# g_norm loaded as a row, chunk 3 token-major: a linear-attention and SoLU kernel with a new order table

## The chip, the cores and the metric

The kernel runs on one core of a Trainium2 chip. The metric is the device time of one execution in microseconds (us): the median of 3 runs is 185.53 us (184.94 to 195.7). One further execution was recorded by the profiler, and every row and time line below is from that one.

The engines are named as in the profile: PE is TensorE (matmuls; PEld its weight loads), DVE is VectorE, ACT is ScalarE, POOL is GpSimd and SP is SyncE, which here only issues transfers.

## The reference

```python
# attention: q, k, v are (8 batches, 8 heads, 576 tokens, 64)
kv  = einsum('bhsd,bhse->bhde', k, v)
out = einsum('bhsd,bhde->bhse', q, kv)
out = out / sqrt(mean(out * out, axis=-1) + 1e-6) * g_norm
x   = out.transpose(0, 2, 1, 3).reshape(4608, 512)
# feed-forward: w_in (512, 1024), w_out (1024, 512)
h    = x @ w_in
e    = exp(h - max(h))
solu = h * e / (sum(e) + 1e-9)
mu, var = mean(solu), mean((solu - mu) ** 2)          # over 1024
y    = ((solu - mu) / sqrt(var + 1e-6) * g_ln) @ w_out
```

All inputs and the result are float32; the kernel computes the matmuls in bfloat16. It leaves the division by the sum of exponentials and the subtraction of the mean out of the large tensors: u = h * exp(h) is multiplied with a w_out whose columns are scaled by g_ln and centred, and one factor per token, made from the sums of u, of its squares and of the exponentials, scales the result.

## The kernel before

**Chunks.** The 4608 tokens are cut into nine chunks of 512: chunks 0 to 7 hold 512 tokens of one batch each, chunk 8 the 64 that are left of every batch. Batches 0 and 1 are loaded in two halves of four heads, the others whole. For the first half of batch 0, q, k and v go through staging tiles that SP loads in float32; all other loads are issued by POOL, which converts to bfloat16 on the way. POOL also issues w_in, w_out and the last tokens of q (`q_last`).

**Attention** of chunk c: `kv_mm` (L376, PE) makes the k-v products of a batch, and copies on DVE or ACT bring them to `kvd`. q is turned, by PE and a copy for chunks 0 to 3 (`qT_mm`, L414), by a DMA transpose that SP issues for chunks 4 to 8 (`qT`, L422). `o_mm` (L433) is the attention product, in two halves. Then, four times per chunk: a square on ACT (`sq`, L236), a mean over the head by a matmul (`s_mm`, L445), the reciprocal root on ACT (`ln` and `ex`, L449 and L453; one instruction, L459, in chunk 0), and `x` on DVE (L465), which multiplies the attention output by the root and by g_norm. For that g_norm stands in a column of 128 partitions, `g_rep`, twice the 64 values; two DMAs write it (L294, L295). g_ln is loaded as eight rows (L293), turned on PE (`turn_g`, L287) and copied by DVE (`g_ln`, L290).

**Feed-forward, feature-major** (chunks 0 to 3): `h` (L502) makes 128 features by 512 tokens with four matmuls, `exp` on ACT (L509), `u` on DVE (L513). For the sums, POOL squares u (`usq`, L238, now and then on ACT, L236) and adds pairs of exponentials (`es`, L526); then 80 narrow matmuls (`sums`, L612) add over features, and a few short DVE instructions (`turn`, `stats`, L619 to L629) make the variance. The output matmuls (`out`, L692) take u as it is.

**Token-major** (chunks 4 to 8, `TOKS`): `h` (L530) makes 128 tokens by 512 features with four matmuls. `expt` on ACT (L538) gives the sum of the exponentials with it, in an accumulator that is read by an instruction of its own. `ut` is on DVE (L544), and `bn` (L550, batch-norm statistics, one per tile of 512) and `stats` (L555 to L561) on DVE replace squares, pair sums and `sums`. u has to be turned for the output: two DMA transposes per chunk on SP (`turnu`, L566).

`rstd` (L633, L635) makes the factor on ACT, `ob` scales the output on DVE or ACT (L244, L242), and SP or ACT stores it.

**Order.** Every piece is a word in `ORDER`, such as `h.5.2.0` or `kv_mm.7.0`, with `:act` where it goes to ACT. `Plan.emit` issues the pieces in exactly that order, so each engine works through its own in the order of the table, and a piece whose input is late holds up all behind it on that engine. `HOME` says which of the eight PSUM banks each product uses, and the tiles have few buffers (k, v, q and qT three, x and u two, e and ob four). `warm` pieces are fillers (`FILL`): matmuls of zeros that PE works on, `("s.warm", 19, 512)` being 19 of them, 512 columns wide, into the bank of that name.

Of the kernel before, what the change touches and what calls it, by code (L numbers as in the profile page):

```python
# [8 lines left out]
FP32 = mybir.dt.float32  # L9
# [26 lines left out]
sq.2.0.1 v.4.0 u.1.7 usq.1.7 qT_mm.3.0 w_center.4 u.1.1 usq.1.6 h.1.2.1 exp.1.2 es.1.1 w_center.7 u.1.2 sums.0 qT.3.0
s_mm.2.0.0 turn.0 ln.2.0.0 ex.2.0.0 out.0.0.2 out.0.0.3 k.4.0 stats.0 out.0.2.0 s_mm.2.0.1 ln.2.0.1 out.0.2.1
out.0.2.2 x.2.0.0 usq.1.2 ex.2.0.1 x.2.0.1 rstd.0 ob.0.0 out.0.3.0 out.0.3.1 o_mm.2.1 sq.2.1.0 kv_mm.3.0 kv.3.0.1
kv.3.1.2 sq.2.1.1 qT_mm.3.1 kv.3.0.0:act kv.3.1.0:act store.0.0 out.0.2.3 kv.3.0.2 ob.0.2 store.0.2 s_mm.2.1.0
out.0.3.2 out.0.3.3 ln.2.1.0 h.2.6.0 s_mm.2.1.1 ob.0.3:act qT.3.1 ex.2.1.0 x.2.1.0 ln.2.1.1 ex.2.1.1 usq.1.5 out.0.1.0  # L40
out.0.1.1 x.2.1.1 out.0.1.2 out.0.1.3 ob.0.1:act store.0.3 h.2.1.0 usq.1.1 kv.3.1.1:act h.2.7.0 kv_mm.4.0 kv.4.1.0:act
kv.4.0.2:act o_mm.3.0 kv.4.0.1:act sq.3.0.0 kv.4.1.1 h.2.1.1 kv.4.1.2 kv.4.0.0 q.4.0 h.2.7.1 h.2.3.0 qT.4 es.1.3
h.2.6.1 exp.2.7 exp.2.6 u.2.7 es.1.0 usq.1.3 h.2.0.0 u.2.6 exp.2.1 u.2.1 h.2.0.1 exp.2.0 u.2.0 h.2.3.1 h.2.5.0 exp.2.3
u.2.3 s_mm.3.0.0 k.5.0 h.2.2.0 ln.3.0.0 h.2.4.0 h.2.2.1 h.2.5.1 ex.3.0.0 x.3.0.0 v.5.0 usq.2.7 exp.2.2 exp.2.5 h.2.4.1
u.2.5 usq.2.5 sq.3.0.1 sums.1 turn.1 stats.1 es.2.3 u.2.2 o_mm.3.1 sq.3.1.0 store.0.1 exp.2.4 out.1.2.0 out.1.2.1
# [5 lines left out]
usq.3.0 x.4.0.1 store.1.1 exp.3.2 u.3.1 h.3.7.1 o_mm.4.1 kv_mm.7.0 exp.3.7 u.3.7 sq.4.1.1 es.3.0 kv.7.1.2 out.2.3.0
u.3.2 usq.2.0 kv.7.0.1 usq.2.6 ex.4.0.0 store.1.0 sq.4.1.0 s_mm.4.1.1 ln.4.1.1 usq.2.1 kv.7.1.0:act v.6.0 out.2.3.1
q.6.0 h.3.3.1 kv.7.1.1 ex.4.1.1 qT.6 kv.7.0.0 es.3.2 exp.3.3 q_last.4 x.4.0.0 u.3.3 s_mm.4.1.0 ln.4.1.0 x.4.1.1
kv.7.0.2:act sums.2 o_mm.5.1 turn.2 stats.2 usq.3.6:act ex.4.1.0 x.4.1.0 o_mm.5.0 sq.5.0.0 sq.5.0.1 es.3.3 rstd.2
sq.5.1.0 ob.2.3 out.2.2.0 out.2.0.0 out.2.0.1 ob.2.0 s_mm.5.0.1 store.2.3 out.2.2.1 ob.2.2 ln.5.0.1 ex.5.0.1 x.5.0.1
s_mm.5.0.0 ln.5.0.0 ex.5.0.0 k.6.0 usq.3.2 usq.3.4 s_mm.5.1.0 h.4.0.1 out.2.1.0 out.2.1.1 ln.5.1.0 expt.4.0.1 ut.4.0.1
es.3.1 x.5.0.0 ex.5.1.0 x.5.1.0 h.4.0.0 usq.3.3 q_last.2 expt.4.0.0 ut.4.0.0 sq.5.1.1 h.4.1.1 expt.4.1.1 ut.4.1.1
h.4.3.1 bn.4.0.1 h.4.2.0 kv_mm.6.0 kv.6.0.1 kv.6.1.2 kv.6.0.2 expt.4.3.1 ob.2.1:act kv.6.0.0 kv.6.1.0 ut.4.3.1
s_mm.5.1.1 q_last.5 ln.5.1.1 h.4.3.0 expt.4.3.0 ut.4.3.0 ex.5.1.1 out.3.0.0 usq.3.7 h.4.1.0 kv.6.1.1 expt.4.1.0
usq.3.5 usq.3.1 ut.4.1.0 sums.3 turn.3 stats.3 expt.4.2.0 o_mm.6.1 sq.6.1.1 sq.6.1.0 x.5.1.1 h.4.2.1 expt.4.2.1  # L60
# [117 lines left out]
def kernel(  # L178
# [13 lines left out]
    nc = tc.nc  # L192
# [595 lines left out]
```

## Time and profile before

| what | value |
|---|---|
| median of 3 runs | 185.53 us (184.94 to 195.7) |
| the profiled execution | 187.05 us, of which 185.2 us are the span from the first to the last instruction |
| granted TensorE clock, mean over the span | 0.978 |
| DVE, ACT, POOL busy | 136.0, 141.3, 81.7 us |
| `usq` on POOL, `es` on POOL | 31 of 1040 ns, 16 of 1272 ns |
| `bn` on DVE | 40 of 682 ns |
| median time from issue to landing of a transpose of q, of u | 8.2 us, 3.9 us |
| HBM read, written | 32.51 MB, 9.44 MB |

How to read it: a line of digits gives 40 equal slices of the span (4.63 us each), each digit the busy share in tenths. A line of a window gives its bounds, its length, then for each engine the busy time and in brackets the number of instructions, then the granted clock as a share of the full one, the mean busy share of the 16 DMA engines and the GB/s moved. A line of waits reads: the engine and piece that waited, an arrow to what it waited for, us in total, times, and the longest. A line of the chain gives the start, the length and the piece that the end of the span hung on. A line of a DMA issue gives the count, the KB of each and the us from issue to landing.

### The profile page before, as it was taken

To read this page: it belongs to the slowest core of one execution; us is meant where nothing else is said; L and a number is where in the kernel's file an instruction comes from. 1 tells how busy PE (TensorE), PEld (TensorE's weight loads), DVE (VectorE), ACT (ScalarE), POOL (GpSimd) and SP (SyncE) were. 2 spreads that over 40 slices of the span, in tenths; PEclk is the share of its full clock that TensorE was granted. 3 is DMA by queue.
4 is the path that set the end of the run, shared out by engine and by line. 5 is a ranking of instruction groups with operands and counts; after the bars stand their busy time and mean duration, and the time that the engine had idled before them with its cause. 6 is when DMAs were issued, how large, how long until landed. Compare 5 with 4: busy or idle time off the path is not lost.

```text
span 185.2 us, 4994 instructions
## 1 busy us (share of the span) xinstructions
PE 172.4 (93%) x1996; PEld 86.2 (47%) x2019; DVE 136.0 (73%) x281; ACT 141.3 (76%) x281; POOL 81.7 (44%) x94
## 2 busy tenths in 40 slices
PE   7959999999996999986999999999999999999992
PEld 2545546545453454433544554444444444444451
DVE  1132879999974774673676989799999799988921
ACT  2205999998885989993899879989998987636541
POOL 7832169989999259959999600000000000000000
PEclk9997999999999999996999999999999999999998
DMA  5999999999999999999999996995977394199984
GB/s 191 277 156 206 223 306 321 207 170 190 195 155 240 185 170 167 204 137 264 173 219 137 211 225 98 271 208 127 224 162 172 70 235 96 43 255 212 237 224 169
DMA packets 55320, 35.80 MB, mean 193 GB/s; under 512 B 37240, under 2 KB 49024, under 8 KB 55296
## 3 DMA queue, kind: packets, MB, share of 16 engines
q0 software_dynamic: 17264, 16.45, 54.8%
q1 hardware_dynamic: 37600, 18.36, 43.8%
q10 hardware_dynamic: 432, 0.66, 1.0%
q8 instruction: 16, 0.26, 0.6%
q14 instruction: 8, 0.07, 0.1%
HBM read 32.51 MB, written 9.44 MB: 227 GB/s over the span
## 4 chain that ended last, share of the span: by engine, by line
PE 60%; DMA 14%; POOL 10%; DVE 7%; issue 4%; ACT 3%; POOLq 0%; DVEq 0%
PE out_ps L692 27%; PE h_ps L530 19%; DMA v_sb<-in_v_dram 10%; PE h_ps L502 5%; DMA k_sb<-in_k_dram 4%; POOL usq_sb L238 4%; POOL es_sb L526 3%; PE s_ps L445 3%; PE misc_ps L376 2%; ACT e_sb L509 2%; DVE x_sb L465 2%; PE o_ps L433 2%; DVE misc_ps L663 2%; DVE u_sb L513 1%; POOL k_sb L312 1%
## 5 line engine op out<-in xcount | busy, mean ns | idle before, releaser
L238 POOL TENSOR_TENSOR usq_sb<-u_sb 128x512 bf16<-128x512 bf16 x31 | 31.7, 1040 | 13.8 <-DVE u_sb L513 11.5
L530 PE MATMUL h_ps<-w_in_sb,x_sb 128*128 128x512 bf16 x156 | 37.3, 379 | 0.2
L692 PE MATMUL out_ps<-w_out_sb,w_sb 128*128 128x512 bf16 (+1 forms) x163 | 36.1, 369 | 0.3
L465 DVE SCALAR_TENSOR_TENSOR x_sb<-o_ps,g_rep,rst_sb 128x512 bf16<-128x512 f32 x36 | 26.3, 745 | 9.3 <-ACT rst_sb L453 7.6
L538 ACT ACTIVATE e_sb<-h_ps,zero_t 128x512 f32<-128x512 f32 x40 | 27.2, 685 | 6.2 <-PE h_ps L530 6.1
L692 PE MATMUL out_ps<-w_out_sb,u_sb 128*128 128x512 bf16 x122 | 30.8, 385 | 0.6 <-issue 0.2
L502 PE MATMUL h_ps<-x_sb,w_in_sb 128*128 128x512 bf16 x122 | 29.8, 379 | 0.6 <-issue 0.5
L544 DVE TENSOR_TENSOR u_sb<-h_ps,e_sb 128x512 bf16<-128x512 f32 x40 | 26.4, 682 | 4.3 <-ACT e_sb L538 4.2
L449 ACT ACTIVATE lss_sb<-s_ps,eps_t 128x512 f32<-128x512 f32 x32 | 21.9, 685 | 6.7 <-PE s_ps L445 6.5
L550 DVE BATCH_NORM_STATS2 bn_sb<-u_sb 128x6 f32<-128x512 bf16 x40 | 25.8, 682 | 0.2
L692 PEld LDWEIGHTS <-w_sb 128*128 128x128 bf16 x168 | 16.3, 98 | 18.1 <-issue 0.2
L513 DVE TENSOR_TENSOR u_sb<-h_ps,e_sb 128x512 bf16<-128x512 f32 x32 | 20.9, 684 | 4.7 <-ACT e_sb L509 4.7
L236 ACT ACTIVATE osq_sb<-o_ps,zero_t 128x512 bf16<-128x512 f32 x36 | 23.5, 683 | 0.8 <-PE o_ps L433 0.4
L530 PEld LDWEIGHTS <-x_sb 128*128 128x128 bf16 x160 | 15.4, 98 | 18.6 <-issue 0.6
L453 ACT ACTIVATE rst_sb<-lss_sb,zero_t 128x512 f32<-128x512 f32 x32 | 22.8, 722 | 0.6
L509 ACT ACTIVATE e_sb<-h_ps,zero_t 128x512 f32<-128x512 f32 x32 | 20.5, 689 | 1.2 <-PE h_ps L502 0.7
L526 POOL TENSOR_TENSOR es_sb<-e_sb 128x512 bf16<-128x512 f32 x16 | 20.3, 1272 | 1.0 <-ACT e_sb L509 0.9
L692 PEld LDWEIGHTS <-u_sb 128*128 128x128 bf16 x128 | 12.5, 100 | 15.2 <-issue 1.7
L242 ACT ACTIVATE ob_sb<-out_ps,rstd_sb 128x512 f32<-128x512 f32 (+1 forms) x20 | 13.5, 675 | 6.8 <-PE out_ps L692 3.4
L502 PEld LDWEIGHTS <-w_in_sb 128*128 128x128 bf16 x128 | 11.9, 98 | 13.8 <-issue 0.6
L244 DVE TENSOR_SCALAR ob_sb<-out_ps,rstd_sb 128x512 f32<-128x512 f32 (+1 forms) x17 | 12.2, 730 | 6.6 <-PE out_ps L692 3.8
L376 PE MATMUL misc_ps<-v_sb,k_sb 64*64 64x64 bf16 x720 | 8.7, 203 | 5.6 <-DMA v_sb<-in_v_dram 4.2
(75 smaller groups left out, 171.8 us busy)
## 6 DMA issues: line engine op xcount, KB each, us to landing
out_dram<-ob_sb SPq DMA_DIRECT2D x65, 128.0 KB, 2.8
k_sb<-in_k_dram POOLq DMA_DIRECT2D x6, 576.0 KB, 8.0
v_sb<-in_v_dram POOLq DMA_DIRECT2D x6, 576.0 KB, 7.9
q_sb<-in_q_dram POOLq DMA_DIRECT2D x6, 512.0 KB, 7.8
w_sb<-in_moe_w_out_dram POOLq DMA_DIRECT2D x2, 1024.0 KB, 14.5
w_in_sb<-in_moe_w_in_dram POOLq DMA_DIRECT2D x2, 512.0 KB, 13.9
k_sb<-in_k_dram POOLq DMA_DIRECT2D x3, 288.0 KB, 15.1
v_sb<-in_v_dram POOLq DMA_DIRECT2D x3, 288.0 KB, 14.0
```

Source lines behind the costliest of these rows:

```text
L236: nc.scalar.activation(out=dst, in_=src, func=AF.Square, bias=zero_t[:, :])
L238: on[engine].tensor_tensor(out=dst, in0=src, in1=src, op=MUL)
L453: nc.scalar.activation(out=t.rearrange("p a b c -> p (a b c)"), in_=T["lss", i][:, :], func=AF.Exp, scale=-0.5, bias=zero_t[:, :])
L465: nc.vector.scalar_tensor_tensor(out=t[:, 2 * hf:2 * hf + 2, z], in0=T["o", c, hf, z][:, :, :, :], scalar=g_rep[:, :], in1=T["rst", (c, hf ...
L502: nc.tensor.matmul(bank(("h", c, f), [128, 512])[:, :], w_in_sb[:, dt, f * 128:(f + 1) * 128], T["x", c][:, dt].rearrange("p a b c -> p (a ...
L509: nc.scalar.activation(out=t[:, f % 2, :], in_=T["h", c, f][:, :], func=AF.Exp, bias=zero_t[:, :])
L526: on[engine].tensor_tensor(out=t[:, n, :], in0=e[:, 0, :], in1=e[:, 1, :], op=ADD)
L530: nc.tensor.matmul(bank(("h", c, m, g), [128, 512])[:, :], T["x", c][:, dt, m // 2, 2 * (m % 2):2 * (m % 2) + 2, :].rearrange("p b c -> p ...
L538: nc.scalar.activation(out=t[:, g, :], in_=T["h", c, m, g][:, :], func=AF.Exp, bias=zero_t[:, :], accum_out=se[:, m, g:g + 1])
L544: nc.vector.tensor_tensor(out=t[:, m, g * 512:(g + 1) * 512], in0=T["h", c, m, g][:, :], in1=T["e", c, m][:, g, :], op=MUL)
L550: nc.vector.bn_stats(out=t[:, m, g, :], in_=T["u", c][:, m, g * 512:(g + 1) * 512])
L692: nc.tensor.matmul(bank(key, [128, d_model])[:, cols], T["w", c][:, m, f, :] if c in TOKS else T["u", c][:, f, m * 128:(m + 1) * 128], w_o ...
```

## The change

g_norm is no longer written into a column by DMA. It is loaded twice, as a row of 64, into a ninth row beside the eight of g_ln; the turn on PE takes all nine rows, and one copy on DVE gives `g_cols`, whose columns 0 to 7 are g_ln and whose column 8 is g_norm. `x` now needs that copy (`g_ln`) instead of the loads (`gs`).

`TOKS` gains chunk 3: its feed-forward goes the token-major way, with eight `bn`, two `turnu` and no `usq`, `es` and `sums`. Its q is still turned on PE. The order table, the bank table and the fillers are new throughout: 9 filler pieces instead of 13. Among what moves: SP issues the small loads ahead of q's staging load; POOL issues k, q and v of the second half of batch 0, then k and v of batch 1's first half, then both halves of w_in, and only then q of batch 1; the first attention product stands ahead of the second `kv_mm` of batch 0; `kv_mm.5` and `kv_mm.7` stand ahead of `o_mm.3.1` and `o_mm.4.0`; and the stores of chunk 0 stand behind `qT.4` on SP.

```diff
-q.0.1 warm.0 ld.v ld.k k.0.0 v.0.0:act ld.q ident q.0.0 k.0.1 gs warm.1 kv_mm.0.0 v.0.1 warm.4 qT_mm.0.0 kv.0.0.1:act
+warm.3 k.0.1 warm.0 ld.k ld.v q.0.1 warm.2 gs k.0.0 ident warm.1 v.0.1 ld.q v.0.0:act kv_mm.0.0 q.0.0 kv.0.0.1 k.1.0
+qT_mm.0.0 v.1.0 qT_mm.0.1 qT.0.0 kv.0.0.0 o_mm.0.0 w_in.0 kv_mm.0.1 sq.0.0.1 kv.0.1.0 w_in.1 q.1.1 qT.0.1 warm.5
...
+ln.3.0.0 h.2.5.0 h.2.5.1 kv.4.0.1:act kv_mm.5.0 q.4.0 h.2.4.0 h.2.4.1 exp.2.5 u.2.5 kv.5.1.0 o_mm.3.1 qT.4 kv.5.1.1
+store.0.0 store.0.3 usq.1.7:act ex.3.0.0 usq.1.6:act k.7.0 kv.5.1.2 x.3.0.0 kv.5.0.2:act usq.1.1 store.0.2 h.2.7.1
...
-FILL = {0: ("s.warm", 19, 512), 1: ("misc.kv.0.0.1", 18, 128), 2: ("o.0.0.1", 2, 512), 3: ("s.0.0.0", 3, 512), 4: ("misc.kv.0.1.1", 6, 128), 5: ("o.0.1.1", 3, 512), 6: ("h.0.2", 2, 512), 7: ("misc.kv.1.0.1", 3, 128), 8: ("s.1.0.0", 2, 512), 9: ("misc.kv.1.1.1", 33, 128), 10: ("o.1.1.1", 2, 512), 11: ("h.1.0", 1, 512), 12: ("misc.qT.2.1", 6, 128)}
+FILL = {0: ("s.warm", 19, 512), 1: ("misc.qT.0.0", 15, 128), 2: ("o.0.0.1", 2, 512), 3: ("s.0.0.0", 3, 512), 4: ("o.0.1.1", 2, 512), 5: ("h.0.5", 1, 512), 6: ("misc.kv.1.1.1", 21, 128), 7: ("o.1.1.1", 1, 512), 8: ("misc.qT.2.1", 9, 128)}
...
-TOKS = (4, 5, 6, 7, 8,)
+TOKS = (3, 4, 5, 6, 7, 8,)
...
-    g_rep = big.tile([128, 1], FP32, name="g_rep")
-    g_ln_sb = big.tile([128, NF], FP32, name="g_ln_sb")
-    g_rows = big.tile([NF, 128], FP32, name="g_rows")
+    g_cols = big.tile([128, NF + 1], FP32, name="g_cols")
+    g_ln_sb, g_rep = g_cols[:, 0:NF], g_cols[:, NF:NF + 1]
+    g_rows = big.tile([NF + 1, 128], FP32, name="g_rows")
...
     def load_gs(_):
-        nc.sync.dma_start(g_rows[:, :], moe_g_ln.rearrange("(n p) -> n p", p=128))
-        nc.sync.dma_start(g_rep[:64, :], g_norm[:, None])
-        nc.sync.dma_start(g_rep[64:128, :], g_norm[:, None])
+        nc.sync.dma_start(g_rows[0:NF, :], moe_g_ln.rearrange("(n p) -> n p", p=128))
+        for r in range(2):
+            nc.sync.dma_start(g_rows[NF:NF + 1, 64 * r:64 * r + 64], g_norm[None, :])
...
-                add(("x", i), "dve", lambda _, i=i: x_mul(*i), [("ex", i), "gs"], [("o", *i), ("rst", i), ("x", c)])
+                add(("x", i), "dve", lambda _, i=i: x_mul(*i), [("ex", i), "g_ln"], [("o", *i), ("rst", i), ("x", c)])
```

More of the change, by code (lines that the diff above doesn't have):

```diff
@@ L36 @@
[L36 to L45, printed above, removed]
@@ L51 @@
[L51 to L60, printed above, removed]
@@ new lines @@
+h.3.3.1 sq.5.0.1 ex.4.1.1 bn.3.2.1 usq.2.5 sums.2 x.4.1.1 store.1.3 s_mm.5.0.0 expt.3.3.1 turn.2 stats.2 out.2.2.0
+out.2.2.1 q_last.1 ln.5.0.0 rstd.2 ut.3.3.1 bn.3.3.1 turnu.3.0 o_mm.5.1 sq.5.1.1 q.7.0 ex.5.0.0 turnu.3.1 ob.2.3
+store.2.3 x.5.0.0 out.2.1.0 out.2.1.1 sq.5.1.0 ob.2.1 s_mm.5.0.1 ln.5.0.1 h.4.2.0 s_mm.5.1.1 bn.3.0.1 bn.3.2.0
+ex.5.0.1 x.5.0.1 s_mm.5.1.0 ln.5.1.0 q_last.5 ex.5.1.0 x.5.1.0 expt.4.2.0 ln.5.1.1 ex.5.1.1 out.2.0.0 out.2.0.1
+kv_mm.6.0 kv.6.1.1:act kv.6.0.1 kv.6.0.0 qT.7 ob.2.2 store.2.2 h.4.2.1 h.4.0.0 kv.6.0.2 kv.6.1.0:act kv.6.1.2
```

156 lines of the change are left out of this document (84 added, 72 removed).

## The prediction

> **What bounds the kernel now.** I read the page's shares first, then the windows by stage, then the waits of TensorE, then the chain of waits around each of them.
>
> ```profile
> PE 172.4 (93%) x1996; PEld 86.2 (47%) x2019; DVE 136.0 (73%) x281; ACT 141.3 (76%) x281; POOL 81.7 (44%) x94
> PE   7959999999996999986999999999999999999992
> ```
>
> TensorE (PE) is busy for 93% of the span, and the slices that are not full stand at the start, at the 13th, and at the 18th and 19th. The same by stage (the columns are PE, PEld, DVE, ACT, POOL busy, granted clock, DMA share, GB/s):
>
> ```profile
> 13.10:22.00 8.90, 8.48 (x135) 5.26 (x136) 4.48 (x9) 5.70 (x10) 2.18 (x3) 0.81 1.17 209
> 22.00:40.00 18.00, 17.33 (x265) 9.70 (x268) 16.06 (x26) 16.92 (x28) 15.07 (x15) 1.00 1.14 258
> 40.00:60.00 20.00, 18.28 (x393) 9.74 (x396) 15.55 (x32) 16.25 (x35) 19.31 (x21) 1.00 1.12 194
> 60.00:74.00 14.00, 13.90 (x220) 6.92 (x219) 9.17 (x19) 13.28 (x24) 8.02 (x9) 1.00 1.18 175
> 74.00:100.00 26.00, 23.49 (x269) 11.47 (x265) 16.13 (x34) 21.72 (x40) 23.66 (x25) 0.93 1.26 199
> 100.00:176.00 76.00, 75.53 (x571) 34.86 (x579) 69.71 (x145) 62.32 (x140) 4.81 (x7) 1.00 0.86 175
> ```
>
> From 100 us on PE has no gap left: only less PE work can shorten that stage, and VectorE (DVE) stands at 92% beside it. From 22 to 40 us DVE (89%) and ScalarE (ACT, 94%) are nearly full; much of what PE does there is fillers. From 40 to 60 and from 74 to 100 GpSimd (POOL) is the full one, and there PE loses 1.7 and 2.5 us. The waits of PE say on what:
>
> ```profile
> PE misc_ps L376 <- DMA v_sb<-in_v_dram: 4.2, 2, 2.2
> PE misc_ps L376 <- DMA k_sb<-in_k_dram: 1.3, 1, 1.3
> ```
>
> and the chain that ended last, around the second and third of them:
>
> ```profile
> 50.51 8.00 DMA k_sb<-in_k_dram
> ...
> 76.40 8.32 DMA v_sb<-in_v_dram
> 84.72 0.14 issue
> 84.86 1.18 PE misc_ps L376 x60
> ```
>
> k and v products wait for loads that POOL issued late (50.51 and 76.40 us), behind its squares (L238, 1040 ns each) and pair sums (L526, 1272 ns). Two of these waits cost twice:
>
> ```profile
> 9.70:13.10 3.40, 1.31 (x39) 1.08 (x27) 1.31 (x3) 0.27 (x1) 0.77 (x1) 1.00 0.97 152
> 13.10:16.50 3.40, 2.98 (x90) 2.38 (x91) 0.70 (x2) 1.53 (x3) 1.23 (x2) 0.50 1.16 210
> ...
> 81.40:84.80 3.40, 1.39 (x13) 0.44 (x11) 2.50 (x4) 3.36 (x6) 3.40 (x4) 1.00 1.28 150
> 84.80:88.20 3.40, 3.12 (x77) 1.93 (x79) 1.27 (x3) 0.14 (x1) 3.39 (x5) 0.50 1.06 268
> ```
>
> After a stretch in which PE was busy for 1.3 to 1.4 of 3.4 us, the next 3.4 us have half the clock, so 1.7 us of work is lost. The Trainium skill, TensorE: Matmul & The Clock Gate, section "What's actually happening", gives the throttle as following at least one idle window of about 3.4 us; this trace differs, since 2.1 us idle in such a stretch were enough. By that rule the waits below would cost no clock, and the sum below would be 0.9 us lower.
>
> **The change, part by part.** Row durations back to back: 216 ns for a 512-wide matmul (0.86 us for four), 0.66 for an exponential, 0.65 for a product or a statistics instruction on DVE, 1.02 and 1.26 for POOL's two kinds, 0.8 for a load's issue.
>
> *g_norm as a row.* Two column loads that land after 7.5 and 8.2 us become two row loads on the same SP queue, now ahead of q's staging load; that load moves from 1.76 to about 3.5 us, but k's staging landed at 6.0 and q's at 9.4, so on one queue it is not the issue that is late. Cost 0; if q's cast came later by all of 1.75 us, it would be +1.7. The turn is one matmul (271 ns, now 9 rows instead of 8), the copy on DVE 157 ns. x now waits for that copy, which stands directly ahead of the first x on DVE, with every later DVE piece behind it; the wait for the reciprocal root hides it (DVE waits 1.7 us for that there now). 0; without that cover the matmul and the copy, +0.4.
>
> *Start, to 40 us.* The first attention product goes ahead of the second k-v product, whose v load lands at 13.1 in both. That fills the gap before 13.1 and saves the half clock. w_in's first half is issued behind two more k/v loads; its halves landed at 17.7 and 21.9, 2.1 and 2.8 us after the load ahead of each, and by the sizes now ahead I put the first near 18.5, so the first h product starts near 18.7 instead of 19.9: -1.2. Against it, the two q loads of batch 1 now land behind both halves of w_in, at 24 to 25 instead of 15.6 and 19.2, and the q turns stand in PE's queue ahead of the fifth h product: +1 to +2 of wait with the exponentials behind it. Fillers behind 13.2 us go from 13x512 and 42x128 to 4x512 and 30x128: 13x0.216 + 42x0.06 = 5.3 down to 2.7 us. None of this is gained, as the stage is paced by DVE and ACT, whose pieces are the same. Adding up PE's pieces behind 40 us in both tables (0.86 for four matmuls, 0.71 for a k-v product, 0.34 for an attention product, 0.47 for a q turn, 1.23 for sums) gives 133.8 us before and some 133.4 after. I take 0 for the stage; -1.2 to +3 are its ends.
>
> *Chunk 3 token-major.* Goes: on PE 80 narrow matmuls (1.23 us in the chain), on POOL 7 squares and 4 pair sums (7x1.02 + 4x1.26 = 12.2 us), on ACT one square, on DVE the turn and the short statistics (1 us). Three squares of chunks 0 and 1 go from POOL to ACT (+1.4 there with the one gone), so POOL loses 15 us in all. Comes: 8 statistics on DVE (5.2), 4 aggregations and three short ones (1.1), 8 accumulator reads on ACT (203 ns, but exponentials follow each other in 0.66 us with them, so 0), two transposes on SP (3.9 us to landing, some 2 us of SP each). DVE gains 6 us net with the casts and evictions that move; 74 to 100 us has 26 - 16.1 = 9.9 us of DVE idle to take it. I count +0.5; its ends are 0 and the full 6.
>
> *Loads and the turned q.* k.3 is issued near 32 instead of 50.5, v.7 near 60 instead of 76.4. So the waits of 1.3 us (57.3) and 2.1 us (82.8, with the 1.7 of half clock) go: -5.1. What is late next is q of batch 4. On POOL, ahead of it and behind w_out, stood 15 squares, 6 pair sums and 8 loads (15.3 + 7.6 + 6.4 = 29.3 us; issue at 54.3); now 10, 8 and 10 (10.2 + 10.1 + 8.0 = 28.3), with a later exponential ahead of the first pair sum. It is issued about 54.8, no earlier, and now right behind v.5, with k.7 and v.7 behind it. Then it is turned on SP, and the first attention product of chunk 4 needs it:
>
> ```profile
> q_sb<-in_q_dram POOLq DMA_DIRECT2D x1, 512.0 KB, 8.9
> ...
> qT_sb<-q_sb SPq DMA_TRANSPOSE x1, 10.3
> ...
> v_sb<-in_v_dram POOLq DMA_DIRECT2D x1, 576.0 KB, 11.0
> ```
>
> Before, the load (8.9) ended at 63.2 and the turn (10.3) at 73.6; the product ran at 73.73, so nothing was spare. The third row is the second of two loads issued 0.8 us apart: 11.0. After: 54.8 + 11.0 + 10.3 = 76.1; with the row of the lone load 74.0, with the shortest q load of that size (5.5) and the other turn (9.6) under 72. I take 76.1, as the pair is the nearest row. PE would be there by 72.7: pieces up to the product add up to 59.4 us against 62.8 before, less the waits gone, plus those above.
>
> **Sum.** PE's work from that product on is 103.2 us in the old table (166.0 - 62.8) and 102.9 in the new one (162.3 - 59.4). Before: 73.7 + 103.2 + 4.7 lost (2.1 + 1.7 + 0.9 small) = 181.7, where PE ends; eviction and store make it 185.2. After: 76.1 + 102.9 + 0.9 (half of a half-clock stretch behind a wait of 3.4 us) + 0.3 to 1.8 for chunk 5's q (issued after a square that needs chunk 2's product; I take 0.9) + 0.9 small + 0.5 DVE = 182.2, and 3.5 of tail: 185.7. Against the span of 185.2 that is +0.5; the profiled execution took 187.05 with what lies around its span, so 187.5. The median of the runs shown is 185.53, 1.5 below that; the forecast on its scale is 186.0. As the walk adds waits at their longer rows I lower it by half of the 2.1 us that lie between the pair's row and the lone load's: **185.0**, no change. 2% (3.7 us) is about what a measurement of this kernel can tell from none.
>
> **The rivals.** *The turned q is in time* (27%): if q lands as fast as a lone load or the turn takes 8.2 us (the median of the four), PE runs on at 72.7: 72.7 + 102.9 + 0.9 + 0.9 + 0.5 + 3.5 = 181.4, 3.8 below the span before; with the start's gain kept 180.2. For it: POOL's relief and the earlier k and v. Against: two more loads in flight at that time.
>
> *DVE becomes the bound* (16%): statistics of chunk 3 stand in DVE's queue ahead of x of chunk 4's second half and of chunk 5. If a statistics instruction delays an x that PE wants next, its 0.65 us is paid, and behind 100 us there is only 8% left to catch up. With 4 to 6 of the 6 us paid on top of the forecast: 189 to 191. It decides once DVE lags PE by more than the products that PE has in store, some 4 us of output matmuls. For it: 92% there now. Against: PE lost 0.5 us of 76 with it.
>
> *The start starves PE* (9%): q of batch 1 lands 3 us after PE wants it and the fillers are gone, so a stretch at half clock follows: +3 + 1.7 into a stage paced by ACT and DVE, 188 to 190.
>
> *POOL's relief moves nothing* is the forecast itself (48%): waits for loads give way to waits for turned q, 183 to 187.5.
>
> **How the numbers follow.** Faster by over 2% (below 181.8): most of the first rival, 0.25. Slower (above 189.2): most of the two slow ones and a tail of the forecast, 0.22. Within: 0.53. Range 179.5 to 190.
>
> **What would show it.** Right: the attention product of chunk 4 waits 2 to 4 us for a transpose, half clock behind it, k-v products wait under 1 us, POOL ends near 90 us. The DVE step is wrong if PE falls below 97% behind 100 us; the start if the first h product comes after 20 us; the forecast if that transpose lands by 73 us.

## The result, and the profile after

The changed kernel takes **195.69 us** (median of 4 runs, 194.58 to 197.71), the kernel before beside it 185.79 us. The ratio is **1.053 (95% interval 1.043 to 1.063)**: slower by 5%, where no change was forecast. From one execution to the next the kernel before took 184.8 to 198.6 us in all that follows, the longer ones mostly at a lower granted clock, so ratios, and times called undisturbed, leave those out. The profiled execution took 194.99 us, 193.2 of them the span (before: 187.05 and 185.2).

The page's shares and PE's slices, after:

```profile
PE 171.6 (89%) x1912; PEld 82.0 (42%) x1912; DVE 141.9 (73%) x293; ACT 142.5 (74%) x289; POOL 66.3 (34%) x80
PE   7968997899999999499984299999998999999990
```

PE has as much work as before in a longer span, DVE has 5.9 us more and POOL 15.4 less, as forecast. The gaps are other ones: those at the 13th, 18th and 19th slice are gone, and new ones stand at the 17th and at the 22nd and 23rd (near 77 and near 106 us). The 7 and 8 between 29 and 39 us are short waits, the longest of 0.71 us, in a stretch that has fewer fillers than before. By stage (PE, PEld, DVE, ACT, POOL busy, granted clock, DMA share, GB/s):

```profile
13.10:22.00 8.90, 7.64 (x143) 3.43 (x131) 4.27 (x9) 6.67 (x11) 1.48 (x2) 1.00 1.16 224
22.00:40.00 18.00, 15.76 (x196) 8.92 (x194) 17.29 (x27) 17.21 (x29) 16.00 (x17) 1.00 1.17 258
40.00:60.00 20.00, 19.70 (x403) 10.33 (x402) 17.19 (x35) 18.83 (x39) 17.06 (x18) 1.00 1.20 201
60.00:74.00 14.00, 14.00 (x289) 6.80 (x288) 10.29 (x25) 12.96 (x26) 5.19 (x6) 1.00 1.17 195
74.00:100.00 26.00, 23.23 (x262) 10.38 (x261) 19.40 (x35) 20.25 (x42) 17.60 (x20) 0.93 1.25 204
...
113.00:188.20 75.20, 74.52 (x430) 34.05 (x429) 63.26 (x136) 58.65 (x133) 0.00 (x0) 1.00 0.79 155
100.00:113.00 13.00, 6.05 (x27) 2.07 (x25) 5.94 (x11) 4.42 (x12) 0.00 (x0) 0.75 1.40 183
```

From 40 to 74 us PE now misses 0.3 us (before: 1.8). The first attention product of chunk 4 (`o_mm.4.0`) runs at 70.57 us instead of 73.73: up to there the change is **3.2 us ahead**. From that product to PE's last matmul before took 107.9 us (73.73 to 181.66); after takes 118.1 (70.57 to 188.71). The two ends, of before and then of after (start, length, piece):

```profile
73.73 0.41 PE L433 MATMUL o_ps<-qT_sb,kvd 64*64 64x256 bf16 x8
...
171.98 9.68 PE L692 MATMUL out_ps<-w_out_sb,w_sb 128*128 128x512 bf16 x52
```

```profile
70.57 0.41 PE L433 MATMUL o_ps<-qT_sb,kvd 64*64 64x256 bf16 x8
...
177.74 10.97 PE L692 MATMUL out_ps<-w_out_sb,w_sb 128*128 128x512 bf16 x58
```

All of the loss is in that part, and behind 113 us nothing is wrong: 74.5 of 75.2 us busy. What ended PE's two long waits, and the two DVE waits behind them:

```profile
PE h_ps L530 <- DVE u_sb L544: 5.8, 1, 5.8
PE h_ps L530 <- DVE ob_sb L244: 3.8, 2, 2.7
```

```profile
DVE ob_sb L244 <- DMA out_dram<-ob_sb: 7.9, 4, 3.5
...
DVE u_sb L544 <- DMA w_sb<-u_sb: 6.1, 1, 6.1
```

The rows of waits for v and k that were shown of before have no counterpart: no k-v product waits for a load any more. The chain that ended last says where the two stops are (start, length, piece):

```profile
71.06 7.81 DMA out_dram<-ob_sb
79.00 0.76 DVE ob_sb L244
79.81 1.88 PE h_ps L530 x4
...
91.16 9.60 DMA out_dram<-ob_sb
100.95 0.69 issue
101.67 7.22 DMA w_sb<-u_sb
109.01 0.70 DVE u_sb L544
109.76 1.87 PE h_ps L530 x4
```

**The first stop.** An eviction of chunk 1 (`ob`, four buffers) waits on DVE for a store of chunk 0 that is in flight until 79.0 us; a PSUM bank comes free late, and PE stands for 2.7 us. **The second stop.** A u of chunk 4 waits on DVE for a DMA that turns u: the transposes of chunk 3's u, which the change adds. Both stops are followed by the half clock:

```profile
76.50:79.90 3.40, 0.74 (x4) 0.29 (x3) 0.90 (x2) 1.37 (x4) 3.40 (x4) 0.88 1.13 216
79.90:83.30 3.40, 3.40 (x11) 1.21 (x11) 2.49 (x5) 1.53 (x5) 3.38 (x5) 0.62 1.22 129
102.60:106.00 3.40, 1.40 (x13) 0.55 (x13) 0.30 (x1) 1.47 (x3) 0.00 (x0) 1.00 1.70 159
106.00:109.40 3.40, 0.00 (x0) 0.00 (x0) 0.39 (x1) 0.00 (x0) 0.00 (x0) 0.56 1.19 225
109.40:112.80 3.40, 3.04 (x8) 1.08 (x8) 3.37 (x7) 1.14 (x3) 0.00 (x0) 0.50 1.03 203
```

The first costs 2.7 us idle and 0.38 x 3.4 = 1.3 of clock; the second leaves 7.0 of the 13 us from 100 to 113 idle (5.8 for u, and 1.2 ahead of it for an eviction), and 0.5 x 3.04 = 1.5 of clock. Together 12.5 us. The wait for v and its half clock, which cost the same part 3.8 us before, are gone, and the part has grown by 10.2 us, so some 1.5 us are left that were not followed up.

Why the turn of u is late stands on SP's queue. After, the transposes that SP issues (start, time on the queue):

```profile
62.46 5.36 SPq L422 DMA_TRANSPOSE qT_sb<-q_sb  x1
78.68 4.04 SPq L422 DMA_TRANSPOSE qT_sb<-q_sb  x1
84.11 6.34 SPq L422 DMA_TRANSPOSE qT_sb<-q_sb  x1
93.16 13.67 SPq L566 DMA_TRANSPOSE w_sb<-u_sb  x2
```

The first transpose of u of the kernel before, and the landing of the two in the kernel after (DMA issues from 88 to 112 us):

```profile
113.56 2.05 SPq L566 DMA_TRANSPOSE w_sb<-u_sb  x1
```

```profile
w_sb<-u_sb SPq DMA_TRANSPOSE x2, 14.1
```

Two transposes, of which one took 2 us of the queue before, hold it for 13.67, and land after 14.1 us where the median before was 3.9. In flight beside them are the eight loads of the last q rows (`q_last`), which POOL issues from 84.9 to 95.0 us and which take 14.1 us to landing in the median:

```profile
84.91 0.80 POOL L334 DMA_DIRECT2D q_last<-in_q_dram  x1
...
86.43 2.98 POOL L334 DMA_DIRECT2D q_last<-in_q_dram  x4
...
94.23 0.74 POOL L334 DMA_DIRECT2D q_last<-in_q_dram  x1 [0.48 <-DMA q_last<-in_q_dram]
```

Before, POOL issued them from 88.7 to 104.8 us, and no turn of u came before 113.6.

### The profile page after: what moved, and what is told of

Read it like the earlier page. It is cut to its first block, busy times and chain, and to the rows that moved or that the text cites. A ratio compares the mean times of both kernels' runs of the same rounds, so it can differ in the third digit from the quotient of the medians.

```text
span 193.2 us, 4804 instructions
## 1 busy us (share of the span) xinstructions
PE 171.6 (89%) x1912; PEld 82.0 (42%) x1912; DVE 141.9 (73%) x293; ACT 142.5 (74%) x289; POOL 66.3 (34%) x80
## 4 chain that ended last, share of the span: by engine, by line
PE 42%; DMA 25%; ACT 12%; DVE 10%; issue 3%; SPq 3%; POOL 2%; DVEq 0%; ACTq 0%; POOLq 0%
PE h_ps L530 17%; PE out_ps L692 16%; DMA out_dram<-ob_sb 12%; DMA w_in_sb<-in_moe_w_in_dram 7%; PE h_ps L502 5%; DMA w_sb<-u_sb 4%; ACT e_sb L509 3%; DMA qT_sb<-q_last 2%; SPq L710 2%; DVE x_sb L465 2%; ACT lss_sb L449 2%; ACT rst_sb L453 2%; PE s_ps L445 2%; PE o_ps L433 2%; DVE u_sb L544 1%
## 5 line engine op out<-in xcount | busy, mean ns | idle before, releaser
L530 PE MATMUL h_ps<-w_in_sb,x_sb 128*128 128x512 bf16 x192 | 48.7, 397 | 9.6 <-DVE u_sb L544 5.8
L692 PE MATMUL out_ps<-w_out_sb,w_sb 128*128 128x512 bf16 (+1 forms) x200 | 44.4, 371 | 0.0
L530 PEld LDWEIGHTS <-x_sb 128*128 128x128 bf16 x192 | 19.0, 101 | 34.3 <-issue 14.9
L550 DVE BATCH_NORM_STATS2 bn_sb<-u_sb 128x6 f32<-128x512 bf16 x48 | 31.7, 682 | 0.2
L465 DVE SCALAR_TENSOR_TENSOR x_sb<-o_ps,g_cols,rst_sb 128x512 bf16<-128x512 f32 x36 | 26.4, 744 | 6.0 <-ACT rst_sb L453 4.5
L238 POOL TENSOR_TENSOR usq_sb<-u_sb 128x512 bf16<-128x512 bf16 x21 | 21.7, 1044 | 17.6 <-DVE u_sb L513 17.5
L502 PE MATMUL h_ps<-x_sb,w_in_sb 128*128 128x512 bf16 x96 | 23.7, 380 | 1.4 <-DMA w_in_sb<-in_moe_w_in_dram 0.7
L692 PE MATMUL out_ps<-w_out_sb,u_sb 128*128 128x512 bf16 x96 | 23.4, 380 | 0.0
L526 POOL TENSOR_TENSOR es_sb<-e_sb 128x512 bf16<-128x512 f32 x12 | 15.3, 1273 | 1.6 <-ACT e_sb L509 1.4
L445 PE MATMUL s_ps<-osq_sb,head_mean 128*128 128x512 bf16 x36 | 13.1, 387 | 0.9 <-ACT osq_sb L236 0.8
L692 PEld LDWEIGHTS <-u_sb 128*128 128x128 bf16 x96 | 8.9, 98 | 10.5 <-issue 0.6
## 6 DMA issues: line engine op xcount, KB each, us to landing
v_sb<-in_v_dram POOLq DMA_DIRECT2D x3, 288.0 KB, 10.2
```

Source lines behind the costliest of these rows:

```text
L238: on[engine].tensor_tensor(out=dst, in0=src, in1=src, op=MUL)
L465: nc.vector.scalar_tensor_tensor(out=t[:, 2 * hf:2 * hf + 2, z], in0=T["o", c, hf, z][:, :, :, :], scalar=g_rep, in1=T["rst", (c, hf, z)][ ...
L502: nc.tensor.matmul(bank(("h", c, f), [128, 512])[:, :], w_in_sb[:, dt, f * 128:(f + 1) * 128], T["x", c][:, dt].rearrange("p a b c -> p (a ...
L530: nc.tensor.matmul(bank(("h", c, m, g), [128, 512])[:, :], T["x", c][:, dt, m // 2, 2 * (m % 2):2 * (m % 2) + 2, :].rearrange("p b c -> p ...
L550: nc.vector.bn_stats(out=t[:, m, g, :], in_=T["u", c][:, m, g * 512:(g + 1) * 512])
L692: nc.tensor.matmul(bank(key, [128, d_model])[:, cols], T["w", c][:, m, f, :] if c in TOKS else T["u", c][:, f, m * 128:(m + 1) * 128], w_o ...
```

## The experiments

Several chips were used, and each ratio is held against executions of before on the same chip. The line numbers of the kernels differ by one to three. The changed kernel itself varied little and was measured again among them as the yardstick (`c_after`):

> The changed kernel once more, unaltered, so that the other runs of this group have it beside them on the same chip. Both theories: 194 to 197 us, 2 to 6% above the kernel before.

Measured: 196.04 us (195.0 to 196.9), ratio 1.042 (1.033 to 1.051).

### Is it the buffer of u?

u has two buffers. By the addresses of the tiles, chunk 4's u is given the one of chunk 3's u in the changed kernel, not that of chunk 2's: the last readers of chunk 3's u, its transposes, stand in the order ahead of `out.2.0.1`, the last reader of chunk 2's. That is why chunk 4 waits for transposes at all. A third buffer takes the wait away, and leaves the transposes as they are:

```diff
-"e": 4, "u": 2, "usq": 2, "es": 2,
+"e": 4, "u": 3, "usq": 2, "es": 2,
```

> The changed kernel with three buffers for u instead of two, nothing else. Theory: in the changed kernel the products of chunk 4 wait 6.1 us on VectorE for the transposes of chunk 3, because u of chunk 4 was given the buffer of u of chunk 3 (both lie at one address) and not that of chunk 2; with a third buffer that wait is gone, TensorE's gap of 7.2 us near 103 to 110 us closes and with it a stretch of half clock: 184 to 187 us. Rival: the transposes of chunk 3 land after 14 us instead of 3.9 and hold SP's queue, whatever the buffer; the wait then only moves to chunk 3's output products and to the q turn of chunk 7, and no more than 3 us come back: 191 to 194 us.

Measured: 188.73 us (186.82 to 189.61), 7.3 below the changed kernel on the same chip. The row `DVE u_sb <- DMA w_sb<-u_sb` is gone, PE is busy for 11.07 of the 13 us from 100 to 113 (6.05), and the transposes are as slow as they were:

```profile
94.27 13.77 SPq L566 DMA_TRANSPOSE w_sb<-u_sb  x2
```

So it is the hand-over of the buffer that costs: no wait of PE of 0.3 us or more names the transposes in this kernel. The forecast (184 to 187) was missed by 1.7 us, as other waits are left: at the first stop 2.2 us for an x and 0.6 for an eviction, and at 102.7 us 1.9 for another eviction. The same with no buffer added, by two words of the order:

```diff
-rstd.2 ut.3.3.1 bn.3.3.1 turnu.3.0 o_mm.5.1 sq.5.1.1 q.7.0 ex.5.0.0 turnu.3.1 ob.2.3
+rstd.2 ut.3.3.1 bn.3.3.1 o_mm.5.1 sq.5.1.1 q.7.0 ex.5.0.0 ob.2.3
...
-out.2.0.0 out.2.0.1 kv_mm.6.0
+out.2.0.0 out.2.0.1 turnu.3.0 turnu.3.1 kv_mm.6.0
```

> The changed kernel with the two transposes of chunk 3's u placed later in the order, behind the last output product of chunk 2 that reads chunk 2's u (out.2.0.1), and nothing else: no further buffer. The u of chunk 4 is then given the buffer of chunk 2's u, and that of chunk 5 the one of chunk 3's u. My theory, that the hand-over of the buffer is what let the slow transposes stop TensorE: the wait of chunk 4's u for them (6.1 us) and the idle TensorE behind 102 us go as they went with a third buffer of u; 5 to 9 us below the changed kernel, 187 to 191 us where that one takes 196. The rival, that the late landing itself costs, whoever has the buffer: the wait turns up at chunk 3's output products or at chunk 5's u, within 3 us of the changed kernel, 193 or more.

Measured: 189.18 us (187.66 to 190.61, ten runs), ratio to before 1.010 (1.003 to 1.017). SP's queue and PE's waits in this kernel:

```profile
96.04 13.35 SPq L565 DMA_TRANSPOSE w_sb<-u_sb  x2
```

```profile
PE h_ps L529 <- DVE ob_sb L243: 5.3, 2, 2.7
PE o_ps L432 <- DMA qT_sb<-q_sb: 1.5, 1, 1.5
```

The transposes are again slow (13.35 us), the wait of u for them is gone, and what is left of PE's long waits are two for evictions, of 2.6 us at 79.6 us (the first stop) and of 2.7 at 103.0, and one for a turned q. The theory holds: the order of two words in the table, which decides who gets which buffer, is worth some 7 of the 10 us (this kernel and `c_after` ran on different chips).

### Why are these transposes slow?

Theory: because of the loads of the last q rows, which pick one row of 64 values out of nine and so move small pieces. First those loads were issued earlier, at 58 to 70 us:

```diff
-h.2.2.0 h.2.2.1 usq.1.5 v.7.0 usq.1.2 sums.1
+h.2.2.0 h.2.2.1 usq.1.5 v.7.0 usq.1.2 q_last.1 q_last.5 q_last.6 q_last.3 q_last.7 q_last.0 q_last.2 q_last.4 sums.1
```

> The changed kernel with the eight loads of the last tokens of q issued by GpSimd while it idles near 59 us instead of near 85 to 95 us. Theory: the transposes of chunk 3 take 14.1 us to land because these loads, which move 64 KB each in pieces of 256 bytes, are in flight with them; moved, the transposes land within 4 to 6 us, the wait for the buffer of u is at most 1 us, and the time is 186 to 189 us (less what the q turn of chunk 4 loses to them). Rival: it is the other load of q and the stores, or two transposes at once, that slow them; then they still take over 10 us and the time stays at 193 to 196 us.

Measured: 193.76 us (192.99 to 193.99). The two transposes now took 6.56 us on SP and landed after 6.4, and chunk 4's u waited 1.8 us instead of 5.8 (PE's row). But the loads now stood in the way elsewhere: PE waits 4.1 us for turned q of chunks 4 and 5, and the gain is 2.3 us only: the forecast (186 to 189) was missed. Then they were held back instead, in the changed kernel and with nothing else altered:

```diff
+    add("gate", "pool", lambda _: nc.gpsimd.tensor_copy(gate_t, T["x", 5][:, 2, 1, 0, 0:1]),
+        [("x", (5, 1, 1))], [("x", 5)])
...
-kv.6.1.2 expt.4.2.1 x.5.1.1 ut.4.2.1
+kv.6.1.2 expt.4.2.1 x.5.1.1 gate q_last.1 q_last.5 ut.4.2.1
```

> The changed kernel with one thing more: a copy of one column of chunk 5's attention output on POOL, behind which stand all eight loads of the last q rows, so that they go out at some 98 us instead of 85 to 94. Buffers and order otherwise as in the change; chunk 4's u still has chunk 3's buffer. My theory, that these loads slow the two transposes of chunk 3's u: those take 4 to 6 us on SP instead of 13.7 and land within 7, chunk 4's u doesn't wait, the second stop of TensorE at 102 to 110 us is gone, the first at 77 to 80 stays: 186 to 190 us where the changed kernel takes 196. The rival, that the transposes are slow of themselves (their shape, or what else is in flight there): 10 us or more to land again, 193 or more.

Measured: 191.49 us (190.18 to 193.24), 4.5 below `c_after`, which ran on another chip. Its transposes on SP:

```profile
95.75 6.37 SPq L568 DMA_TRANSPOSE w_sb<-u_sb  x2
```

and what the DMA queues did, of the changed kernel from 92 to 108 us and of this one from 92 to 101.8 us (packets, MB, share of 16 engines' time):

```profile
q1 hardware_dynamic: 5770, 1.90, 78.4%
q0 software_dynamic: 4520, 1.02, 71.1%
```

```profile
q1 hardware_dynamic: 4395, 1.55, 93.5%
q0 software_dynamic: 465, 0.46, 27.6%
```

With POOL's loads beside them (q0: 4520 packets of 226 bytes in the mean), SP's transfers (q1) move 1.90 MB in 16 us; without them 1.55 MB in 9.8 us, and the two transposes take 6.37 us instead of 13.67. So the company of these loads is a little over half of the time, shown by moving them ahead and by holding them back. What makes up the rest is open: in the changed kernel the next pair of turns, at 113.50 us, takes 7.43 us on SP with no load of POOL in flight. The Trainium skill, DMA: Bandwidth & Descriptors, section "Queues, rings and completion order", says that an engine takes turns between the queues packet by packet; these rows agree with that, though no run here shows the turns one by one. The forecast for this run (186 to 190) was missed by 1.5 us: the second stop shrank, from 5.8 us of waiting to 2.6, and did not vanish, since the transposes landed after 6.3 us, still more than the 3.9 of before. The other row is the first stop: at 78.4 us an attention product waits for an x that stands on DVE behind an eviction.

```profile
PE o_ps L432 <- DVE x_sb L464: 2.9, 1, 2.9
PE h_ps L532 <- DVE u_sb L546: 2.6, 1, 2.6
```

### The first stop: stores, and what is behind them

Theory: the stores of chunk 0, which the new order puts behind the turn of chunk 4's q on SP, keep the output tiles. Put right behind their evictions, alone and with three buffers of u:

```diff
-out.0.0.3 rstd.0 ob.0.0:act s_mm.2.0.1
+out.0.0.3 rstd.0 ob.0.0:act store.0.0 s_mm.2.0.1
```

(the same for the other three)

> The changed kernel with the four stores of chunk 0 right behind their evictions in the order table, so ahead of the q turn of chunk 4 on SP. Theory: VectorE's wait of 3.5 us near 75 to 79 us is for a buffer that a store of chunk 0 still reads, as that store stood behind the q turn; the gap of 2.7 us on TensorE and the half clock behind it go, and the wait near 103 us stays: 190 to 192 us. Rival: the stores are slow because the loads and transposes in flight take the DMA engines, not because of their place; then the wait moves to the next store and the time stays at 194 to 196 us.

> Both edits of the two runs before together: three buffers for u, and the stores of chunk 0 ahead of the q turn. Theory: the two waits are all that the changed kernel loses, and what is left is a gain of about 4 to 6 us against the kernel before (loads issued earlier, no wait of the k-v products, no sums of chunk 3): 179 to 182 us. Rival: VectorE, with 6 us more to do, or the slow transposes bound the second half, and the time stays above 185 us.

Measured: 201.55 us (197.71 to 203.13) and 191.89 us (190.32 to 192.76). Undisturbed they took 197.71 (one execution) and 190.3 to 192.8, without the move 195.0 to 196.9 and 186.8 to 189.6: no better in the first case and worse in the second, so this theory of the cure fell. In the second kernel PE waits for loads of k again:

```profile
PE misc_ps L375 <- DMA k_sb<-in_k_dram: 3.8, 2, 3.3
PE h_ps L529 <- DVE ob_sb L243: 2.9, 1, 2.9
```

It seems that stores issued sooner delay the loads that fly beside them; that was not tested by itself. Then eight output tiles instead of four, alone and with three buffers of u:

```diff
-"ob": 4, "us": 1,
+"ob": 8, "us": 1,
```

> The changed kernel with eight buffers for the evicted output instead of four, and nothing else; the stores stay where they are. Theory: VectorE's waits of 3.5, 1.6 and 2.8 us are for buffers whose stores of the chunk before land late, not for the stores' place in the table (moved ahead they only delayed the loads of k); with four more buffers the gap of 2.7 us near 77 us and its half clock close, and the wait for u near 103 us stays: 189 to 192 us. Rival: what is late there is all of the DMA traffic, and with the gap gone TensorE reaches the next late transpose earlier and waits there: 194 to 196 us.

> The changed kernel with three buffers for u and eight for the evicted output. Theory: with both kinds of wait gone the changed kernel shows what the change saves otherwise, 1.2 us of sums and the waits of the k-v products: 181 to 184 us, 1 to 3% below the kernel before. Rival: the turned q of chunk 5 (waited 0.6 us at 88 us in the run with three buffers for u) and the transposes of chunk 3 (14 us to landing) take over the wait: 186 to 189 us.

> Three buffers of u and eight output tiles alone, as in e6_u3_ob8, beside the three above: 186 to 188 us, with the one wait of some 5.7 us for chunk 5's turned q and TensorE at half clock behind it. If it stands within 1 us of the three above, moving that load is worth nothing, whatever the waits show.

Measured: 196.36 us (195.98 to 196.53) alone, ratio 1.044 (1.037 to 1.051); with three u 187.02 (185.03 to 190.13), ratio 0.986 (0.973 to 0.999), and on the second occasion 186.63 (185.41 to 189.75). The ratio on record for that second occasion, 0.956, stands against executions of before near 194.9 us; beside the undisturbed ones on that chip (184.8 to 186.1) the kernel is level. Alone, eight tiles are worth nothing: the rival (194 to 196) was right, and in `e6_u3_ob8` as well (186 to 189). PE's first two rows with eight tiles alone:

```profile
PE o_ps L433 <- DMA qT_sb<-q_sb: 4.5, 1, 4.5
PE h_ps L530 <- DVE u_sb L544: 4.4, 1, 4.4
```

The waits for stores are gone, and in their place PE waits 4.5 us for the turned q of chunk 5: that q was late all along, as its turn lands at 87.8 us in the changed kernel and at 87.6 here, and the store hid it. With three u as well that is the only long wait left (4.2 us on the second occasion). The same buffers in the order of before:

> The kernel before with the same additional buffers, three for u and eight for the evicted output. Theory: the waits for these buffers come with the new order, so here the buffers change nothing: within 1% of the kernel before. Rival: the kernel before loses as much to them (its VectorE and ScalarE waited 4.9 us in all for stores) and gains 2 us or more, so that the order is not to blame.

Measured: 192.48 us (189.21 to 197.42), ratio 1.013 (0.992 to 1.033). The old order does not gain from them, so they cure something that the new one brought.

### Can the late q of chunk 5 be cured?

POOL issues it at 69.8 us, behind a square that waits 10 us for u of chunk 2. Placed ahead of that square (58.3 us), its turn ahead of chunk 1's stores, in the changed kernel and in the one with more buffers:

```diff
-v.7.0 usq.1.2 sums.1
+v.7.0 usq.1.2 q.5.0 sums.1
...
-ex.4.0.1 x.4.0.1 usq.2.0 store.1.0
+ex.4.0.1 x.4.0.1 usq.2.0 qT.5 store.1.0
```

> The changed kernel with its buffers as they are, and q of chunk 5 loaded earlier: its load stands on POOL's queue right behind the square usq.1.2 (about 59 us) instead of behind usq.2.2, which waits 10 us for its u (69.8 us); its transpose stands ahead of the first store of chunk 1 on SP. My theory: chunk 5's attention no longer waits for its turned q at all, but the first stop, at 77 to 80 us, comes from a store's buffer and the second, at 102 to 110 us, from the transposes of chunk 3's u; both stay for the most part: 0 to 3 us below the changed kernel, 193 to 196 us. The rival, that the late q of chunk 5 also made these stops: 188 or less.

> The changed kernel with three buffers of u, eight of the output tile, and chunk 5's q loaded earlier as in e10_q5. With the buffers alone 187.0 us were measured, with one wait of 5.8 us left, that of chunk 5's attention for its turned q. My theory: that wait is a late issue, and goes with it: 3 to 6 us below, 181 to 184 us, 2 to 4% below the kernel before. The rival: the load of q now flies beside the turn of chunk 4's q and the loads of chunk 7's k, which come later for it by as much, as happened when other loads were put there: 186 us or more, and a wait for chunk 4's turned q or for k in place of the one removed.

Measured: 195.36 us (193.36 to 197.17) and 186.23 us (185.70 to 187.42), the second with a ratio of 0.984 (0.971 to 0.996) to before. Each is within 1 us of its kernel without the move: as expected in the first, where the two stops stayed, and against the theory in the second, whose rival was right. There the wait moved to chunk 4's q, whose turn the load now meets; the chain of that kernel has it:

```profile
62.03 10.59 DMA qT_sb<-q_sb
72.62 0.04 issue
72.67 0.41 PE o_ps L432 x8
```

10.6 us instead of the 8.6 and 8.2 of the two runs with the buffers alone. So the load was put between the two, at 64 and 67 us, with POOL's squares and pair sums that were ready ahead of it; once more with the order of `e11_turnu` in place of a third u; and once more with the loads of the last q rows held back behind `x.4.1.1`:

```diff
-v.7.0 usq.1.2 sums.1
+v.7.0 usq.1.2 es.2.0 usq.2.6 usq.2.0 usq.2.1 usq.2.5 usq.2.7 usq.2.4 q.5.0 sums.1
```

(`e13_q5_late`; in `e12_q5_mid` the load stands behind `usq.2.1`)

> Three buffers of u, eight output tiles; POOL's four pieces of work that are ready (es.2.0 and the squares of u.2.6, u.2.0, u.2.1, some 4.4 us) stand behind usq.1.2, then the load of chunk 5's q, which so goes out near 62.7 us (69.3 with the buffers alone, 58.3 in e9_u3_ob8_q5), then the other squares; its transpose ahead of the first store of chunk 1. My theory, that the wait is a late issue and nothing else: load landed by 72, turned by 81, chunk 4's turn undisturbed: 182 to 184.5 us, PE's waits for turned q under 1 us. The rival, that the load disturbs chunk 4's turn wherever it flies beside it: a wait of 1.5 us or more for chunk 4's turned q, and 185 to 187.

> As e12_q5_mid, with three more squares ahead of the load, which goes out near 65.8 us. Theory: beside chunk 4's turn for 5 us only, landed by 75, turned by 83: 182 to 185 us, at most 1.5 us of waiting for chunk 5's turned q. The rival, that the queue of transposes is what is slow: 4 us or more of waiting for a turned q as with the buffers alone, 185 to 188.

> As e13_q5_late with two buffers of u, but with the two transposes of chunk 3's u placed behind out.2.0.1, so that chunk 4's u gets chunk 2's buffer: order and eight output tiles alone, no third buffer of u. Theory: the same as e13_q5_late within 1 us. The rival, that the third buffer does more than let chunk 4's u past the transposes: 2 us or more slower, with a wait of DVE for chunk 3's transposes in chunk 5's u.

> As e13_q5_late (three buffers of u, eight output tiles, chunk 5's q loaded at 67 us), with the loads of the last q rows held back by the same kind of copy, of chunk 4's attention output: they go out at 84 us or later, as in the change, instead of 76. My theory: the turn of chunk 5's q, issued at 74.5, takes 6 us on SP instead of 8.9 and lands by 83; TensorE waits at most 1.5 us for it: 182 to 185 us. The rival, that turned q of chunk 5 is late however early it is loaded: a wait of 4 us or more as with the buffers alone, 186 or more.

Measured: 196.92 us (193.86 to 199.37), 194.44 (190.64 to 195.99), 194.67 (192.37 to 195.84) and 195.31 (189.40 to 196.22); undisturbed 195.4, 192.7, 194.5 and, in one execution, 189.4, beside the 186.0 of the buffers alone. All four forecasts (182 to 185) were missed, by 4 to 11 us. In `e12_q5_mid` the rival was right: beside the loads of q that POOL issued at 63.96 and 69.31 us, the turn of chunk 4's q took 16.7 us to landing, and PE waited 8.6 us for it. In `e13_q5_late` and `e14_turnu_q5_late` POOL, done with its squares sooner, issued the loads of the last q rows from 76 us on instead of 85, into the turns of chunks 5 and 6; in `e14_turnu_q5_late`:

```profile
74.95 8.23 SPq L421 DMA_TRANSPOSE qT_sb<-q_sb  x1
85.86 8.40 SPq L421 DMA_TRANSPOSE qT_sb<-q_sb  x1
```

8.2 and 8.4 us on SP, where the changed kernel has 4.0 and 6.3, and PE waits 7.6 us for turned q, 5.9 of them for chunk 5's. Holding those loads back (`e16_q5_gate`) did not help: the loads of chunk 6's k and v went out at 75 to 76 us, as in the two runs before it, instead of 81 to 83, the turn of chunk 5's q took 7.67 us on SP, and PE waited 5.3 us. The theory of a late issue fell. What is left of the loss behind the hand-over is a stretch from 60 to 105 us in which transfers share the DMA engines without a gap (the windows above give a DMA share of 1.17 to 1.40 there), and each load that was moved there made another transfer late; that the sharing itself is the cause is argued, not shown. An order of loads that avoids it was not found.

### The row of g_norm alone

The kernel before with g_norm loaded and turned as rows (as in the diff of the change), and nothing else of the change but `g_ln` a few words earlier, which x then needs:

```diff
-sq.0.0.0 s_mm.0.0.0 warm.5 kv.0.1.1 ex.0.0.1
+sq.0.0.0 s_mm.0.0.0 warm.5 kv.0.1.1 g_ln ex.0.0.1
```

> The kernel before with one part of the change alone: g_norm loaded as rows beside g_ln and turned on TensorE by the same matmul (g_ln's step stands a few places earlier in the order for it); chunk 3, the rest of the order and the buffers as before. My theory: this part is worth at most what the change showed at its start, a first h product some 2 us earlier, of which later waits for loads take most: 0 to 2 us faster than the kernel before in the same group, within 1%. The rival, that this part carries the loss: 3 us or more slower.

Measured: 193.29 us (187.09 to 198.33) beside 192.41 of before; its undisturbed execution took 187.09, those of before 185.94 to 188.48. As far as one undisturbed execution tells, nothing is gained and nothing lost in the end, though its first attention product ran at 12.90 us instead of 14.13 and its first h product at 18.34 instead of 19.91: the 1.6 us are gone again by the waits for v and k, which it still has (2.4 and 2.2 us).

## Why the prediction was wrong

- **g_norm as a row, 0:** right, and so was the sign at the start. The first h product came at 17.73 us (forecast 18.7), and the attention product at 31.80 before came at 30.77; nothing starved. Of this gain and of the k and v waits (forecast -5.1) 3.2 us were in hand at 70.57 us.
- **Waits of the k-v products:** gone, as forecast.
- **The turned q of chunk 4, at 76.1 us:** wrong. It was issued at 53.46, the load took 8.9 and the turn 8.1 us: 70.5. The pair's row (11.0) and the longer turn (10.3) were taken; the lone load's row was the right one. That it landed before 73 us was the forecast's own sign of being wrong, and PE itself was there at 70.57 us and not at 72.7. The first rival, that the turned q is in time, came true at its own place, and the time went the other way all the same.
- **The failed step** is two transposes on SP "3.9 us to landing, some 2 us of SP each", priced at nothing beside the rest of chunk 3. They took 13.67 us on SP and 14.1 to landing, and the second half of the error is in what they hold: the sum asked which engine pays for a transpose, and not whose buffer it keeps. Two steps were missing: that chunk 3's transposes, issued at 93.16 us, meet the loads of `q_last`, which are issued from 84.9 to 95.0 us now and would have been in flight there at their old times too (88.7 to 104.8); and that the order of the last readers gives chunk 4 the buffer of chunk 3. That cost some 7 us by `e1_u3` and `e11_turnu`.
- **Chunk 5's q, +0.9:** right in kind and too small. With the waits for stores out of the way it costs 4.2 to 4.5 us. Its bounds (0.3 to 1.8) came from the square ahead of it; POOL in fact waited 10.0 us there, and the turn's own 9.2 and 10.5 us in the two runs with the buffers alone were hidden by nothing.
- **The stores of chunk 0 behind the turn of chunk 4's q** were seen in the diff and not priced: 2.7 us and the half clock, on the same stretch in which chunk 5's q would have been late.
- **DVE:** the step was right. PE fell to 91% behind 100 us, which was to show it wrong, but through the second stop; behind 113 us it stands at 99%, with 5.9 us more on DVE than before. The rival in which DVE becomes the bound did not happen.
- **The clock:** by the rule of the Trainium skill (TensorE: Matmul & The Clock Gate, "What's actually happening") a whole idle window of about 3.4 us is needed. Neither stop agrees: in windows of 0.1 us the granted clock falls to 0.50 at 79.1 us, after PE had gone idle at 77.1, and at 106.4, after PE had gone idle at 104.0. So 1.9 and 2.4 us were enough, as 2.1 were before, and the prediction was right to price half-clock stretches.

In sum: forecast from `o_mm.4.0` to PE's end 106.1 us (102.9 + 0.9 + 0.9 + 0.9 + 0.5), measured 118.1; the start of that part was forecast 5.5 us too late (76.1, measured 70.57), and the tail is 4.5 us instead of 3.5. The two errors of 12.0 and -5.5 leave 7.5 with the tail's 1.0: 185.7 forecast, 193.2 measured.

No version ran clearly faster than the undisturbed executions of before. The change with three buffers of u and eight output tiles comes out level with those (185.0 to 187.2, before 184.8 to 188.8), and 9 us below the change as it is.

## What to carry to other kernels

When an order table changes, list for every pool with few buffers which tile is released first, and by what kind of reader: a tile whose last reader is a transfer should not be the one that the next chunk gets. Price an added transfer by what flies at that moment, not by its median in a quiet stretch; and when an engine is relieved, ask which transfers it will issue sooner and into what, as `e13_q5_late` and `e14_turnu_q5_late` show. Where one wait is removed and the time stays, look at the next row of the waits: here the store hid a late q.

## What the runs showed of the hardware

Two DMA transposes that hold SP's queue for some 2 us each in a quiet stretch took 13.4 to 13.8 us for the pair beside POOL's loads of small pieces (changed kernel, `e1_u3`, `e11_turnu`), and 6.4 to 6.6 without these loads (`e17_gate`, `e4_qlast`). Moving a single load of 512 KB from 69 to 58 us lengthened the landing of the turn that it met from 8.2 and 8.6 us to 10.6. The granted clock of TensorE fell to half after 1.9 and 2.4 us idle in the changed kernel, and came back 3.4 and 6.8 us later.
